# A Fourier stage with one split group, and earlier loads at the start, in a mixed SSM and GLU kernel

## The chip, the cores and the metric

The kernel runs on one core of one Trainium2 chip. The metric is the device time of one execution in microseconds. A core has one matrix engine (TensorE, PE in the profile; PEld is its weight load) and several others that each run their own instructions in order: VectorE (DVE), ScalarE (ACT), GpSimd (POOL) and SyncE (SP). SP issues most of the transfers, POOL the rest.

## The reference

Two branches work on the same 2048 tokens of width 512 in fp32, each on its own input, and a gate per token mixes them. Branch A is a diagonal state-space model, evaluated as a convolution of length 2048 with a kernel K per channel through Fourier transforms of length 4096. Branch B is a bilinear gated linear unit (GLU) with F = 1792.

```python
def _A_ref(u, log_A_real, A_imag, C_real, C_imag, log_dt, D_skip):   # u: 1 x 2048 x 512, N = 128
    dt = jnp.exp(log_dt)
    A = -jnp.exp(log_A_real) + 1j * A_imag
    C = (C_real + 1j * C_imag) * dt[:, None]
    P = jnp.exp((A * dt[:, None])[:, :, None] * pos[None, None, :])
    K = 2.0 * jnp.einsum("dn,dnl->dl", C, P).real
    Kf, Uf = jnp.fft.rfft(K, 2 * L), jnp.fft.rfft(u_t, 2 * L)
    y = jnp.fft.irfft(Uf * Kf[None, :, :], 2 * L)[:, :, :L]
    return y.transpose(0, 2, 1) + u * D_skip[None, None, :]

def _B_ref(x, w_gate, w_up, w_down):                                 # 512 -> 1792 -> 512
    h = jnp.einsum("bsd,df->bsf", x, w_gate) * jnp.einsum("bsd,df->bsf", x, w_up)
    return jnp.einsum("bsf,fd->bsd", h, w_down)

g = _sigmoid((A_u * gate_w).sum(-1, keepdims=True))
return g * _A_ref(A_u, ...) + (1 - g) * _B_ref(B_x, ...)
```

## The kernel before

**The GLU.** F is cut into 14 blocks of 128, in four groups of 3, 3, 4 and 4 (`GROUPS`). The tokens stand in four columns `ci` of 512. The loop `glu` (L650) goes through the groups, and in each through the columns, up and down by turns. `hidden` makes for each block the products `pg` and `pu` (weights `w_gate` and `w_up` in `whi`, `wlo`) and multiplies them to `h`; `down` multiplies `h` with `w_down` (`dhi`, `dlo`) into `y`; `evacuate` scales `y` by one minus the gate into `acc` on ACT and stores it. Each fp32 number is split in a high and a low part of the faster fp32r format, and each product is three matmuls of 128x128 by 512 columns: `dhi,hl`, `dlo,hh`, `dhi,hh` for `y`, and one with `wlo` and two with `whi` for `pg` and `pu`. The high part is a cast on ACT, the low part a subtraction on DVE. There are 2016 such large matmuls in all. The `w_down` rows of the first group come in three transfers into a tile `kt`.

**Tokens.** In the first group, `tokens` (L520) loads a column's tokens x^T in four pieces `kt`, splits them into `xs`, and stores the split tile to DRAM (`xs_d`) for the later groups, which read it from there. For columns 0 and 1 the test at L664 calls `ahead` (L530) first: it loads the four pieces into two staging tiles `ts`, column 1 from planner time 12 on. Columns 2 and 3 come through the rotating buffer `raw`.

**The convolution.** `u_part` (L691) loads u in four tiles of 1 MB (`in<-in_u`). From each, DVE makes four scores (`y,gate<-in,w3s`, which add up to the gate's input, ACT taking their sigmoid) and the sums for a first Fourier stage. Its results go to DRAM (`su_d`) and come back in another layout for the second stage. DVE and ACT also make tables of powers (`x`, `rt`, `v`) from which PE makes K (k block). `m_second` (L1157) is the second stage: for each of four quarters q of the channels and T = 0 to 3 it fills four PSUM banks with 32x32 by 512-column matmuls, for four row groups `r` (the 32 partitions that hold the operand) and four column groups `c` (the 32 output partitions). For T = 0 and c = 0 each row group's matmul is cut in two halves of 256 columns, one for each p, since the second half needs the weight matrix of index 4 (the insert at L109). Then ACT or DVE empties the banks (`ev`), DVE multiplies the spectra, and two more stages go back. The convolution's matmuls all write tiles named `k` and come in bursts between the large ones. In the trace a burst's fp32 matmul has two records.

**The order.** Nothing is issued as it is written. `add` (in the class `Work`, L170) records a task with its engine, a modelled duration, a rank, the tiles it reads and writes, an earliest time `after` and the size of its transfer. `run` (L268) then simulates all engines: again and again it takes the task with the earliest modelled start, and the tasks are emitted in that order. `InOrder` makes each engine run strictly in it. So a change of one `after` or one duration can change every engine's order from there on, and the chip then keeps to the new order whatever the real times are. L124 is the helper that issues everything, so every row of the profile has that line and the tiles' names tell the rows apart.

Of the kernel before, what the change touches and what calls it, by code (L numbers as in the profile page):

```python
# [10 lines left out]
F32 = mybir.dt.float32  # L11
# [7 lines left out]
P = 128  # L19
# [119 lines left out]
U_STEP = 20.0  # L139
# [185 lines left out]
def gated_mix_kernel(  # L325
# [16 lines left out]
    pe, dve, act, sp, pool_q = (InOrder(tc, e) for e in (nc.tensor, nc.vector, nc.scalar, nc.sync, nc.gpsimd))  # L342
# [3 lines left out]
    add = work.add  # L346
# [173 lines left out]
    def tokens(gi, ci, kt):  # L520

        x = xs[kt] = new("glu", "xs", [P, 2, D], F32R, 5)
        if gi:
            add("sp", 0.42, lambda: sp.dma_start(x.t.bitcast(F32), xs_d[ci, kt]), r=[(m_xs, (ci, kt))], w=[x], dma=512, rank=0)
            return
        load(("x", gi, ci, kt), xT[kt * P : (kt + 1) * P, ci * D : (ci + 1) * D])
        split(x, x, (0, 1), ("x", gi, ci, kt))
        add("sp", 0.42, lambda: sp.dma_start(xs_d[ci, kt], x.t.bitcast(F32)), r=[x], w=[(m_xs, (ci, kt))], dma=512, rank=2)

    def ahead(ci):  # L530

        ts = [load_two(lambda k, n=n: ("x", 0, ci, 2 * n + k), stage, None, False) for n in range(2)]
        for kt in range(KT):
            t, k = ts[kt // 2], kt % 2
            src = xT[kt * P : (kt + 1) * P, ci * D : (ci + 1) * D]
            add("sp", 0.42, lambda t=t, k=k, src=src: sp.dma_start(t.t[:, k], src), w=[(t, k)], dma=256, after=12.0 if ci == 1 else 0.0)

    THREE = ((1, 0), (0, 1), (0, 0))

# [110 lines left out]
    def glu():  # L650
        order = [(gi, ci) for gi in range(len(GROUPS)) for ci in (range(4) if gi % 2 == 0 else range(3, -1, -1))]
        tokens(0, 0, 0)
        weights(GROUPS[0])
        first = new("tab", "kt", [P, 4, D])
        for f in GROUPS[0]:
            raws[("w", f, 2)] = (first, f)
            src = wts[f][:, 2 * D :]
            add("sp", 0.42, lambda f=f, src=src: sp.dma_start(first.t[:, f], src), w=[(first, f)], dma=256, after=9.0 if f == 2 else 0.0)
        down_weights(GROUPS[0])
        old = 0  # L660
        for n, (gi, ci) in enumerate(order):
            fs = GROUPS[gi]
            if ci != old:
                if gi == 0 and ci <= 1:  # L664
                    ahead(ci)
                for kt in range(KT):
                    tokens(gi, ci, kt)
            old = ci
            hs = {f: hidden(f) for f in fs}
            ends = n % 4 == 3 and gi + 1 < len(GROUPS)  # L670
            if ends:
                weights(GROUPS[gi + 1])

            for rr in ((0, 1), (2, 3)):
                ys = {r: new("ps_y", "y", [P, D], bufs=2) for r in rr}
                late = fs[-1:] if rr[0] == 0 else []
                for r in rr:
                    for f in fs:
                        if f not in late:
                            down(ys[r], r, hs[f], wd[f], f == fs[0], f == fs[-1])  # L680
                    if not late:
                        evacuate(gi, ci, r, ys[r])
                if late:
                    for r in rr:
                        down(ys[r], r, hs[fs[-1]], wd[fs[-1]], False, True)
                        evacuate(gi, ci, r, ys[r])
            if ends:
                down_weights(GROUPS[gi + 1])


    def u_part(t):  # L691
        ut = inp([P, 4, D])
        rs = slice(4 * t, 4 * t + 4)
        add("sp", 0.42, lambda: sp.dma_start(ut.t, uv[:, rs, :]), w=[ut], dma=1024, after=9.0 + U_STEP * t)

        def score_of(j):
            r = 4 * t + j
            pr = new("mid", "y", [P, D], bufs=2)
            add(
                "dve", 0.73,  # L700
                lambda: dve.scalar_tensor_tensor(
                    pr.t, ut.t[:, j, :], 1.0, gw.t, op0=ALU.mult, op1=ALU.mult, accum_out=gate[:, r : r + 1]
                ),
                r=[ut, gw], w=[pr, (m_gate, ("s", t))], rank=0,
            )

        for j in range(4):
            score_of(j)
        ones = [new("mid", "y", [P, 2, D], bufs=2) for _ in range(2)]
        ops = (ALU.add, ALU.subtract)  # L710
        for y, op in zip(ones, ops):
            add(
                "dve", 1.22,
                lambda y=y, op=op: dve.tensor_tensor(out=y.t, in0=ut.t[:, :2], in1=ut.t[:, 2:], op=op), r=[ut], w=[y],
            )
        for s, op in enumerate(ops):
            for d, y in enumerate(ones):
                add(
                    "dve", 0.69,
                    lambda d=d, s=s, y=y, op=op: dve.tensor_tensor(  # L720
                        out=ut.t[:, 2 * s + d], in0=y.t[:, 0], in1=y.t[:, 1], op=op
                    ),
                    r=[y], w=[(ut, 2 * s + d)],
                )

        def first(s):
            banks, st = [bank() for _ in range(4)], new("mid", "ev", [P, KT, 4, P], bufs=2)

            def fn():
                for p in range(2):  # L730
                    col, src = 64 * (p + s), 2 * s + (p + s) % 2
                    for tq in range(4):
                        lanes = slice(32 * tq, 32 * tq + 32)
                        pe.matmul(
                            banks[tq].t[64 * p : 64 * p + 64], w1_t.t[lanes, col : col + 64], ut.t[lanes, src],
                            start=True, stop=True, tile_position=(32 * tq, 64 * p),
                        )

            add("pe", 1.3, fn, r=[(ut, 2 * s), (ut, 2 * s + 1), w1_t], w=banks, rank=1, hold=[st])
            for tq in range(4):  # L740
                add(
                    "act", 0.59,
                    lambda tq=tq: act.copy(st.t[:, :, tq], banks[tq].t.rearrange("p (f d) -> p f d", f=KT)),
                    r=[banks[tq]], w=[(st, tq)],
                )
            n0 = 16 * s + 4 * t
            for q in range(KT):
                add(
                    "pool", 0.95,
                    lambda q=q: pool_q.dma_start(  # L750
                        su_d[q, :, n0 : n0 + 4, :], st.t[:, q],
                    ),
                    r=[st], w=[(m_su, (q, n0))], dma=256,
                )

        for s in range(2):
            first(s)
        sc, ga = (m_gate, ("s", t)), (m_gate, t)
        add("act", 1.5, lambda: act.activation(gate[:, rs], gate[:, rs], AF.Tanh, scale=0.5), r=[sc], w=[sc], rank=0)

        def gates():
            dve.tensor_scalar(ngate[:, rs], gate[:, rs], -0.5, 0.5, op0=ALU.mult, op1=ALU.add)
            dve.tensor_scalar(gate[:, rs], gate[:, rs], 0.5, 0.5, op0=ALU.mult, op1=ALU.add)

        add("dve", 0.4, gates, r=[sc], w=[ga, sc], rank=0)
# [391 lines left out]
    def m_second(q, T, ins, w):  # L1157

        banks = [bank() for _ in range(4)]
        to = new("mid", "ev", [P, 2, 2, 2, 2 * P], bufs=2)  # L1160
        at, parts = ins

        def fn():
            src = at().rearrange("l (p c) w d -> l c p (w d)", p=2)
            for c in range(4):
                for r in range(4):
                    lanes, to = slice(32 * r, 32 * r + 32), banks[r].t[32 * c : 32 * c + 32]
                    pieces = [(c, to, src[lanes, c])]
                    if T == 0 and c == 0:

                        pieces = [(4 * p, to[:, 2 * P * p : 2 * P * p + 2 * P], src[lanes, c, p]) for p in range(2)]
                    for m, to, x in pieces:
                        pe.matmul(to, w.t[lanes, m], x, start=True, stop=True, tile_position=(32 * r, 32 * c))

        add("pe", 1.05, fn, r=[*parts, w], w=banks, rank=1, hold=[to], many=apart_of(q))
        for r in range(4):
            h, e = divmod(r, 2)
            evict(
                q, r, 0.59, lambda h=h, e=e: to.t[:, :, e, :, P * h : P * h + P],
                lambda r=r: banks[r].t.rearrange("l (p w d) -> l w p d", p=2, w=2), [banks[r]], [(to, r)],  # L1180
            )
        return to
# [268 lines left out]
```

## Time and profile before

| quantity | value |
|---|---|
| median of 3 runs | 595.36 us (594.47 to 596.06) |
| the profiled execution | 595.34 us |
| its span in the profile | 593.6 us |
| mean granted TensorE clock | 0.996 |
| PE busy | 579.7 us |
| DVE, ACT, POOL busy | 512.1, 401.8, 113.7 us |

The span runs from the first to the last instruction of the profile; the time has 1.7 us around it. A timeline row gives the start, the duration, the engine, the line, the operation with output and inputs, the shape, the count of like instructions in one row, and in brackets the idle time before it with what ended it. Busy times overlap, since matmuls are pipelined, so the pace of PE is read from starts and not from durations. The granted clock is the share of the full TensorE clock.

### The profile page before, as it was taken

To read this page: it belongs to the slowest core of one execution; us is meant where nothing else is said; L and a number is where in the kernel's file an instruction comes from. 1 tells how busy PE (TensorE), PEld (TensorE's weight loads), DVE (VectorE), ACT (ScalarE), POOL (GpSimd) and SP (SyncE) were. 2 spreads that over 40 slices of the span, in tenths; PEclk is the share of its full clock that TensorE was granted. 3 is DMA by queue.
4 is the path that set the end of the run, shared out by engine and by line. 5 is a ranking of instruction groups with operands and counts; after the bars stand their busy time and mean duration, and the time that the engine had idled before them with its cause. 6 is when DMAs were issued, how large, how long until landed. Compare 5 with 4: busy or idle time off the path is not lost.

```text
span 593.6 us, 14891 instructions
## 1 busy us (share of the span) xinstructions
PE 579.7 (98%) x6020; PEld 436.6 (74%) x6020; DVE 512.1 (86%) x812; ACT 401.8 (68%) x891; POOL 113.7 (19%) x159
## 2 busy tenths in 40 slices
PE   8899999999999999899999999999999899999996
PEld 5677676788877777687676877867877776777764
DVE  6998999999998999899999999996999972556845
ACT  5348898898679488878887675799786343433351
POOL 0003212411111231310123201112422104202011
PEclk9989999999999999999999999999999999999999
DMA  8998779896867697998789856899969349898887
GB/s 270 408 368 299 273 274 347 199 309 197 204 178 204 203 239 189 227 267 263 153 200 264 188 149 190 177 279 260 225 137 251 68 131 252 271 285 207 262 187 132
DMA packets 71687, 136.28 MB, mean 230 GB/s; under 512 B 6852, under 2 KB 35780, under 8 KB 69188
## 3 DMA queue, kind: packets, MB, share of 16 engines
q1 hardware_dynamic: 47668, 87.10, 43.0%
q0 software_dynamic: 23392, 47.98, 38.6%
q8 instruction: 47, 0.77, 0.5%
q10 hardware_dynamic: 560, 0.26, 0.2%
q14 instruction: 20, 0.16, 0.1%
HBM read 80.27 MB, written 55.05 MB: 228 GB/s over the span
## 4 chain that ended last, share of the span: by engine, by line
PE 90%; DVE 5%; issue 2%; ACT 2%; DMA 1%; DVEq 0%; SPq 0%; ACTq 0%
PE pg L124 25%; PE y L124 24%; PE pu L124 24%; PE k L124 16%; DVE x L124 1%; DMA y<-in_xT 1%; DVE v L124 1%; DVE wlo L124 1%; DVE in L124 0%; ACT acc L124 0%; DMA raw<-in_xT 0%; DVE h L124 0%; DVE dlo L124 0%; ACT L124 0%; ACT xs L124 0%
## 5 line engine op out<-in xcount | busy, mean ns | idle before, releaser
L124 PE MATMUL pg<-xs,whi 128*128 128x512 f32 x448 | 139.0, 391 | 0.5 <-ACT whi L124 0.5
L124 PE MATMUL pu<-xs,whi 128*128 128x512 f32 x448 | 138.6, 391 | 0.0
L124 PEld LDWEIGHTS pg<-xs,whi 128*128 128x128 f32 x448 | 84.4, 188 | 20.9 <-ACT whi L124 2.1
L124 PEld LDWEIGHTS pu<-xs,whi 128*128 128x128 f32 x448 | 84.4, 188 | 17.0
L124 PE MATMUL y<-dhi,hl 128*128 128x512 f32 x224 | 89.7, 400 | 4.3 <-ACT acc L124 2.2
L124 PE MATMUL pg<-xs,wlo 128*128 128x512 f32 x224 | 89.8, 401 | 2.2 <-issue 1.6
L124 PE MATMUL pu<-xs,wlo 128*128 128x512 f32 x224 | 90.3, 403 | 0.0
L124 PE MATMUL y<-dlo,hh 128*128 128x512 f32 x224 | 87.7, 391 | 0.2 <-DVE dlo L124 0.2
L124 PE MATMUL y<-dhi,hh 128*128 128x512 f32 x224 | 87.5, 391 | 0.0
L124 ACT COPY ev<-k 128x512 f32<-128x512 f32 x112 | 59.4, 599 | 22.6 <-PE k L124 22.5
L124 POOL DMA_DIRECT2D out<-acc x44 | 39.4, 972 | 154.9 <-ACT acc L124 150.3
L124 ACT CAST hh<-h 128x512 fp32r<-128x512 f32 x56 | 34.9, 623 | 45.7 <-DVE h L124 45.0
L124 PEld LDWEIGHTS y<-dhi,hl 128*128 128x128 f32 x224 | 42.0, 188 | 26.8 <-issue 10.6
L124 ACT ACTIVATE acc<-y,ngate 128x512 f32<-128x512 f32 x62 | 42.2, 690 | 27.5 <-PE y L124 24.4
L124 PEld LDWEIGHTS pu<-xs,wlo 128*128 128x128 f32 x224 | 42.1, 188 | 20.9 <-issue 10.5
L124 DVE TENSOR_TENSOR h<-pu,h 128x512 f32<-128x512 f32 x56 | 38.6, 690 | 21.6 <-PE pu L124 19.9
L124 PEld LDWEIGHTS pg<-xs,wlo 128*128 128x128 f32 x224 | 42.3, 189 | 17.0 <-issue 6.2
L124 ACT COPY h<-pg 128x512 f32<-128x512 f32 x56 | 33.0, 590 | 24.6 <-PE pg L124 18.2
L124 PEld LDWEIGHTS y<-dhi,hh 128*128 128x128 f32 x224 | 42.2, 188 | 9.1
L124 PEld LDWEIGHTS y<-dlo,hh 128*128 128x128 f32 x224 | 42.1, 188 | 8.6 <-DVE dlo L124 0.5
L124 DVE TENSOR_TENSOR hl<-h,hh 128x512 fp32r<-128x512 f32 x56 | 38.4, 686 | 4.0 <-ACT hh L124 3.9
L124 POOL DMA_DIRECT2D su_d<-ev x32 | 17.9, 577 | 94.4 <-ACT ev L124 94.4
(130 smaller groups left out, 985.4 us busy)
## 6 DMA issues: line engine op xcount, KB each, us to landing
xs<-xs_d SPq DMA_DIRECT2D x36, 512.0 KB, 6.1
out<-acc POOLq DMA_DIRECT2D x44, 256.0 KB, 5.4
raw<-in_wts SPq DMA_DIRECT2D x33, 256.0 KB, 6.1
xs_d<-xs SPq DMA_DIRECT2D x16, 512.0 KB, 6.0
su_d<-ev POOLq DMA_DIRECT2D x32, 256.0 KB, 6.7
y_d<-ts SPq DMA_DIRECT2D x28, 256.0 KB, 6.0
in<-su_d POOLq DMA_DIRECT2D x12, 512.0 KB, 7.7
sk_d<-ev SPq DMA_DIRECT2D x6, 1024.0 KB, 5.7
```

The costliest lines, as they stand in the source:

```text
L124: got = getattr(self.engine, name)(*args, **kw)
```

## The change

The change has four parts.

- In `m_second` with T = 0, only the first matmul, row group 0 and column group 0, is split. Its half p = 0 (weights 0) comes first, then the 15 whole ones, and its half p = 1 (weights 4) last. The burst has 17 matmuls in place of 20. For T = 1 to 3 nothing changes.
- The stores of column 0's split tokens to `xs_d` may start from planner time 16 + kt on.
- `ahead` is called for column 2 too, from time 42 on; its tokens then go through `ts` and not `raw`.
- The four loads of u may start at 6, 27, 48 and 69 in place of 9, 29, 49 and 69.

```diff
-        add("sp", 0.42, lambda: sp.dma_start(xs_d[ci, kt], x.t.bitcast(F32)), r=[x], w=[(m_xs, (ci, kt))], dma=512, rank=2)
+        add("sp", 0.42, lambda: sp.dma_start(xs_d[ci, kt], x.t.bitcast(F32)), r=[x], w=[(m_xs, (ci, kt))], dma=512, rank=2, after=16.0 + kt if ci == 0 else 0.0)
...
-            add("sp", 0.42, lambda t=t, k=k, src=src: sp.dma_start(t.t[:, k], src), w=[(t, k)], dma=256, after=12.0 if ci == 1 else 0.0)
+            add("sp", 0.42, lambda t=t, k=k, src=src: sp.dma_start(t.t[:, k], src), w=[(t, k)], dma=256, after=12.0 + 30.0 * (ci - 1))
...
-                if gi == 0 and ci <= 1:
+                if gi == 0 and ci <= 2:
                     ahead(ci)
...
-        add("sp", 0.42, lambda: sp.dma_start(ut.t, uv[:, rs, :]), w=[ut], dma=1024, after=9.0 + U_STEP * t)
+        add("sp", 0.42, lambda: sp.dma_start(ut.t, uv[:, rs, :]), w=[ut], dma=1024, after=6.0 + (U_STEP + 1.0) * t)
...
-            for c in range(4):
-                for r in range(4):
-                    lanes, to = slice(32 * r, 32 * r + 32), banks[r].t[32 * c : 32 * c + 32]
-                    pieces = [(c, to, src[lanes, c])]
-                    if T == 0 and c == 0:
-
-                        pieces = [(4 * p, to[:, 2 * P * p : 2 * P * p + 2 * P], src[lanes, c, p]) for p in range(2)]
-                    for m, to, x in pieces:
-                        pe.matmul(to, w.t[lanes, m], x, start=True, stop=True, tile_position=(32 * r, 32 * c))
+            jobs = [(r, c, c, slice(0, 2)) for c in range(4) for r in range(4)]
+            if T == 0:
+
+                jobs = [(0, 0, 0, 0), *jobs[1:], (0, 0, 4, 1)]
+            for r, c, m, p in jobs:
+                lanes = slice(32 * r, 32 * r + 32)
+                to = banks[r].t[32 * c : 32 * c + 32].rearrange("l (p d) -> l p d", p=2)[:, p]
+                pe.matmul(to, w.t[lanes, m], src[lanes, c, p], start=True, stop=True, tile_position=(32 * r, 32 * c))
```

The first place is the start. SP's issues there before, from the second `v` load on (`kt` is the first group's `w_down`, `in` is u's tile, `ts` the second column's tokens, `dt_d` a small table in DRAM):

```order
L124 DMA v<-in_prm 128x1024
L124 DMA kt<-in_wts 128x512 x2
L124 DMA xs_d<-xs 128x1024 x4
L124 DMA in<-in_u 128x2048
L124 DMA kt<-in_wts 128x512
L124 DMA ts<-in_xT 128x512 x4
L124 DMA dt_d<-small 128x4
L124 DMA in<-in_u 128x2048
```

and after the change:

```order
L124 DMA v<-in_prm 128x1024
L124 DMA in<-in_u 128x2048
L124 DMA kt<-in_wts 128x512 x3
L124 DMA ts<-in_xT 128x512 x4
L124 DMA dt_d<-small 128x4
L124 DMA xs_d<-xs 128x1024 x4
L124 DMA x<-dt_d 128x512
L124 DMA in<-in_u 128x2048
```

The four stores of column 0 moved behind u's first tile, all of `kt` and the second column's tokens. DVE at the same place before, from the second block's `hl` on (`x` is the table of powers, `y,gate` a score):

```order
L124 TENSOR_TENSOR hl<-h,hh 128x512
L124 TENSOR_TENSOR dlo<-kt,dhi 128x512 x2
L124 SCALAR_TENSOR_TENSOR x<-x 128x512 x3
L124 TENSOR_TENSOR h<-pu,h 128x512
L124 SCALAR_TENSOR_TENSOR x<-x 128x512 x2
L124 TENSOR_TENSOR hl<-h,hh 128x512
L124 SCALAR_TENSOR_TENSOR x<-x 128x512
L124 SCALAR_TENSOR_TENSOR y,gate<-in,w3s 128x512 x2
L124 TENSOR_TENSOR dlo<-kt,dhi 128x512
```

and after:

```order
L124 TENSOR_TENSOR hl<-h,hh 128x512
L124 SCALAR_TENSOR_TENSOR x<-x 128x512 x3
L124 SCALAR_TENSOR_TENSOR y,gate<-in,w3s 128x512
L124 SCALAR_TENSOR_TENSOR x<-x 128x512
L124 SCALAR_TENSOR_TENSOR y,gate<-in,w3s 128x512
L124 TENSOR_TENSOR dlo<-kt,dhi 128x512
L124 SCALAR_TENSOR_TENSOR y,gate<-in,w3s 128x512
L124 TENSOR_TENSOR dlo<-kt,dhi 128x512
L124 SCALAR_TENSOR_TENSOR y,gate<-in,w3s 128x512
L124 TENSOR_TENSOR dlo<-kt,dhi 128x512
L124 TENSOR_TENSOR h<-pu,h 128x512
L124 TENSOR_TENSOR xs<-ts,xs 128x512
```

The scores moved ahead of the `dlo`, and the first `dlo` now stands behind four `x` and two scores; the third block's `h` and `hl` stand behind all three `dlo`. The second place is the first T = 0 burst on PE, before:

```order
L124 MATMUL pu<-xs,whi 128x512 x2
L124 MATMUL k<-in,w2s 32x256 x8
L124 MATMUL k<-in,w2s 32x512 x12
L124 MATMUL pu<-xs,wlo 128x512
L124 MATMUL pu<-xs,whi 128x512 x2
```

and after:

```order
L124 MATMUL y<-dhi,hh 128x512
L124 MATMUL k<-in,w2s 32x256
L124 MATMUL k<-in,w2s 32x512 x15
L124 MATMUL k<-in,w2s 32x256
L124 MATMUL y<-dhi,hl 128x512
```

The three other row groups lost their halves, the remaining two stand at the burst's ends, and the burst itself stands between other large matmuls. The third place is ACT where the first quarter's second stage is nearly done (T = 2 and 3, about 240 us), before (`ev` empties the banks, `whi` and `wlo` are weights of the next group, `acc` empties `y`):

```order
L124 CAST whi_2966<-raw_2879 128x512
L124 COPY ev_2946<-k_2921 128x2x2x128
L124 CAST whi_2966<-raw_2886 128x512
L124 ACTIVATE rt_2762<-rt_2762,fixed_82 128x672
L124 ACTIVATE wlo_2991<-whi_2966 128x1024
L124 ACTIVATE acc_3017<-y_2942,ngate_84 128x512
L124 ACTIVATE acc_3021<-y_2956,ngate_84 128x512
```

and after:

```order
L124 CAST whi_2964<-raw_2883 128x512
L124 COPY ev_2960<-k_2924 128x2x2x128
L124 COPY ev_2960<-k_2926 128x2x2x128
L124 COPY ev_2960<-k_2928 128x2x2x128
L124 ACTIVATE acc_2985<-y_2915,ngate_84 128x512
L124 CAST whi_2964<-raw_2900 128x512
L124 ACTIVATE acc_2999<-y_2956,ngate_84 128x512
L124 ACTIVATE wlo_3008<-whi_2964 128x1024
```

The two `acc` moved ahead of `wlo`, the first of them also ahead of the second `whi`.

## The prediction

> **What bounds the kernel now.** I read the page's busy times and chain first, then TensorE's waits.
>
> ```profile
> span 593.6 us, 14891 instructions
> PE 579.7 (98%) x6020; PEld 436.6 (74%) x6020; DVE 512.1 (86%) x812; ACT 401.8 (68%) x891; POOL 113.7 (19%) x159
> PE 90%; DVE 5%; issue 2%; ACT 2%; DMA 1%; DVEq 0%; SPq 0%; ACTq 0%
> ```
>
> TensorE (PE) is busy for 98% of the span and is 90% of the chain that ended last. Every microsecond by which it works less, waits less, or runs at a higher clock is a microsecond of the kernel. Next, the waits of PE: releaser, total, times, longest.
>
> ```profile
> PE y L124 <- ACT acc L124: 2.2, 2, 1.5
> PE y L124 <- ACT dhi L124: 2.0, 1, 2.0
> PE pg L124 <- issue: 1.6, 1, 1.6
> PE k L124 <- DVE acc L124: 1.5, 1, 1.5
> PE pg L124 <- ACT whi L124: 1.0, 2, 0.5
> PE k L124 <- DVE v L124: 0.4, 1, 0.4
> PE y L124 <- DVE dlo L124: 0.2, 1, 0.2
> ```
>
> They come to 8.9 us. `dhi` and `dlo` stand at the start, one `acc` of 1.5 in the middle; the first row of `k` and `whi` lie before the place where the orders part.
>
> The busy time itself can shrink too. Here are two second-stage bursts on PE's timeline, with the matmul behind each, the weight loads of the first, and the last burst of its kind.
>
> ```profile
> 201.45 2.13 PE L124 MATMUL k<-in,w2s 32*32 32x256 f32 x40
> 203.51 0.50 PE L124 MATMUL pu<-xs,wlo 128*128 128x512 f32 x1
> 209.87 1.14 PE L124 MATMUL k<-in,w2s 32*32 32x512 f32 x32
> 210.94 0.50 PE L124 MATMUL y<-dhi,hl 128*128 128x512 f32 x1
> ...
> 201.44 1.23 PEld L124 LDWEIGHTS k<-in,w2s 32*32 32x32 f32 x40 [0.35 <-issue]
> ...
> 528.23 2.14 PE L124 MATMUL k<-x,w2s 32*32 32x256 f32 x40
> ```
>
> Two records are one matmul. With T = 0 (20 matmuls) PE moves on after 203.51 − 201.45 = 2.06 us; with T = 1 (16) after 1.07. The four T = 0 bursts, 2.13 to 2.14 long in the records, are alike.
>
> Last, the start: PE's timeline, and two windows (columns PE, PEld, DVE, ACT, POOL busy, granted clock, DMA share, GB/s).
>
> ```profile
> 23.26 0.39 PE L124 MATMUL y<-dhi,hl 128*128 128x512 f32 x1
> ...
> 25.75 0.39 PE L124 MATMUL y<-dhi,hh 128*128 128x512 f32 x1
> 28.10 0.50 PE L124 MATMUL y<-dhi,hl 128*128 128x512 f32 x1 [1.96 <-ACT dhi L124]
> 28.82 0.50 PE L124 MATMUL y<-dlo,hh 128*128 128x512 f32 x1 [0.22 <-DVE dlo L124]
> ...
> 33.03 0.39 PE L124 MATMUL pg<-xs,wlo 128*128 128x512 f32 x1
> ```
>
> ```profile
> 30.00:34.00 4.00, 4.00 (x13) 3.12 (x13) 3.97 (x9) 2.24 (x6) 0.00 (x0) 0.63 0.88 310
> 240.00:250.00 10.00, 8.45 (x65) 6.03 (x64) 8.67 (x11) 9.85 (x18) 3.47 (x4) 1.00 0.84 210
> 20.00:22.00 2.00, 2.00 (x11) 1.65 (x10) 2.00 (x4) 1.15 (x3) 0.00 (x0) 1.00 1.03 422
> ```
>
> Twelve matmuls start from 23.26 to 25.75: (25.75 − 23.26)/11 = 0.227 us each, the full pace. Thirteen start from 25.75 until just before 33.03. They should take 13 × 0.227 = 2.95 and take 7.28, so the start loses 4.3 us. Of that, 1.96 + 0.22 are waits and some 2.0 the lowered clock after them (0.63 in the window from 30 to 34). At 244, a wait of 1.5 left the clock at 1.00.
>
> **The second stage.** The edit removes three of 20 matmuls in each T = 0 burst and moves the second half of the split group to the end. Before, each half's partner on the same tile of the array follows directly. The work of a row group is the same for T = 0 and T = 1 (two halves and three wholes against four wholes), so the 0.99 us of difference are four such pairs, 0.25 each. After the edit no pair is adjacent. Row group 0 runs half a matmul ahead of the others through the middle, and the closing half fills that up. Lower bound: 1.07, as T = 1. Upper bound: the closing half still waits as a pair does and then runs alone as long again, 1.07 + 2 × 0.25 = 1.57. In proportion to matmuls it would be 1.07 + 0.99/4 = 1.32. I take 1.15, a third of a pair's wait over T = 1, because the halves are 15 matmuls apart and nearest to the T = 1 row. Four bursts: 4 × (1.15 − 2.06) = **−3.6 us**, between −4.0 and −2.0. Nothing hides them: PE works on its chain there.
>
> On weights, the row of loads shows all 40 within 1.23 us, while matmuls on the same row groups run until 203.5. [...]
>
> **The start.** SyncE's (SP) issues, the DMA summaries (landings of `kt`; of `in`, median of two), and what VectorE (DVE) and ScalarE (ACT) do with what lands:
>
> ```profile
> 9.85 1.59 SPq L124 DMA_DIRECT2D kt<-in_wts  x2
> 13.30 2.77 SPq L124 DMA_DIRECT2D xs_d<-xs  x4
> 16.13 0.45 SPq L124 DMA_DIRECT2D in<-in_u  x1
> 17.26 0.33 SPq L124 DMA_DIRECT2D kt<-in_wts  x1
> 17.91 3.71 SPq L124 DMA_DIRECT2D ts<-in_xT  x4
> ...
> DMA to landing us min/median/max: 7.4/8.0/10.1
> ...
> in<-in_u SPq DMA_DIRECT2D x2, 1024.0 KB, 10.6
> ```
>
> ```profile
> 19.84 0.69 DVE L124 TENSOR_TENSOR hl<-h,hh 128x512 fp32r<-128x512 f32 x1
> 20.44 1.29 DVE L124 TENSOR_TENSOR dlo<-kt,dhi 128x512 fp32r<-128x512 f32 x2
> 21.64 2.14 DVE L124 SCALAR_TENSOR_TENSOR x<-x 128x512 f32<-128x512 f32 x3
> ...
> 26.84 0.69 DVE L124 SCALAR_TENSOR_TENSOR y<-in,w3s 128x512 f32<-128x512 f32 x1
> ...
> 27.43 0.62 ACT L124 CAST dhi<-kt 128x512 fp32r<-128x512 f32 x1 [2.39 <-DMA kt<-in_wts]
> ```
>
> The third `kt` load is issued at 17.26, behind four stores of 512 KB and u's tile, lands 10.1 later, and PE's 1.96 wait follows. After the change, SP issues u's tile, three `kt`, four `ts`, and only then the stores. The first `kt` landed at 9.85 + 8.0 = 17.9. With u's 1 MB in its place at 422 GB/s (2.5 us in place of 0.6), u lands at about 19.8, the three `kt` at 20.4, 21.1 and 21.7, the `ts` by 24.4. These are estimates from the rows above. ACT then casts the three `dhi` by about 22.5, in time for PE at 23.26, and the wait of 1.96 is gone.
>
> DVE is late next, since its order changes. After `hl` it now does three `x`, a score (`y<-in,w3s`), an `x`, a score, and only then the first `dlo`. At 0.61 per step from row to row (26.84 to the next score, and a third of what two `dlo` and three `x` take) and 0.69 for the last: 20.44 + 3 × 0.69 = 22.5 for the `x`, 24.3 for score, `x` and score, and 24.33 + 0.69 = 25.02 for `dlo`. PE wants it at 23.49, its second matmul, and gets it at 25.07: wait 1.58. The second `dlo` ends at 26.24, in time for 25.07 + 6 × 0.227 = 26.43. PE reaches the next column's products at 27.56 and their low part at 27.79, but DVE's `xs` split ends at about 28.7 (score, `dlo`, `h`, `xs` after 26.16): wait 0.92. The third block's `hl` ends at about 30.2 and costs 0.42. In all 2.92 against 4.3: **−1.4 us**. The longest of these waits is near the 1.5 that left the clock alone at 244, so I count no lowered clock. If only the first wait stays, it is −2.7; if the clock falls as it did at 28, costing 2.0, it is +0.6.
>
> The moved stores cost PE nothing so long as their reader is far: the view of the tile `xs_d` gives
>
> ```profile
> L124 SPq DMA_DIRECT2D xs<-xs_d x36: 319/326/1101, 90.6 to 532.3; - x36
> ```
>
> so the first read back is at 90.6, 60 us behind, and it is column 2's; column 0 comes last of that group. The later u tiles move from 29, 49, 69 to 27, 48, 69 in the planner's time; the third column's four loads keep their bytes and change only the buffer. From 33 to 89 PE has no wait, so neither can gain there. What a loss would be is in the next term.
>
> **The middle.** The planner gives new orders to every engine from the start on, so the waits there are drawn again. The largest, 1.5 at 244, is `acc` standing behind casts on ACT:
>
> ```profile
> 242.43 1.04 ACT L124 ACTIVATE wlo<-whi 128x1024 fp32r<-128x1024 f32 x1
> 243.38 1.25 ACT L124 ACTIVATE acc<-y,ngate 128x512 f32<-128x512 f32 x2
> ```
>
> There both `acc` now stand ahead of `wlo`, and the first also ahead of the second `whi`, so 1.04 of the 1.5 goes. One return from small matmuls to the large ones falls away (PE's order has 61 stretches of products against 62): the rows behind a burst, at 203.51 and 210.94, are 0.50 long against 0.39 in the stream, and I take twice that difference, 0.2. Against this I set one new wait about the size of the other one for `acc` (2.2 − 1.5 = 0.7). Together −1.0 − 0.2 + 0.6 = **−0.7 us**. Bounds: −2.4, all `acc` waits and the switch gone; +1.6, one more wait like the largest. The 1.6 under "issue" waits for nothing that the profile shows; I leave it.
>
> **The sum.** −3.6 − 1.4 − 0.7 = −5.7. The profiled execution took 595.34 (span 593.6 and 1.7 around it), as the median of the runs, 595.36. Forecast: **589.6 us**.
>
> **The rivals.**
>
> *The closing half waits.* The second stage gives −2.0: 591.3. For it: four pairs do cost 0.25 each. Against: the loads' row. Chance 0.12.
>
> *The pauses at the start lower the clock.* Waits of 1.58, 0.92 and 0.42 come within 7 us. For it: 1.96 and 0.22 lowered it at 28. Against: 1.5 at 244 did not. 589.6 + 2.0 = 591.6. [...] Chance 0.15.
>
> *The middle takes the gain back.* Three or four new waits of 1.5 behind casts or loads, as at 244: 594 to 596. For it: DVE is 86% busy and every order is new. Against: before shows only one of that size. Chance 0.09, no measurable difference.
>
> *Slower: DVE waits for u.* The first score now stands ahead of the first `dlo` on DVE and needs u's tile by 22.5. Each microsecond by which u lands later is one of PE's, and 2.0 more for the clock: at 26.7, where u landed before (16.13 + 10.6), 589.6 + 4.2 + 2.0 = 595.8, no faster than before; from 28.1 on it is over 597.15. For it: 10.6 from issue to landing in the summary. Against: issued at 9.85, the same 10.6 ends at 20.5, and the stores no longer stand ahead. Chance 0.06.
>
> **How the numbers follow.** The forecast keeps 0.58. A difference under 0.3% (1.8 us) can't be told from none: 593.57 to 597.15 is the same. Faster: 0.58 + 0.12 + 0.15, less 0.01 for overlaps, 0.84. Same: 0.09 and that 0.01, 0.10. Slower: 0.06. The terms' bounds, taken as independent (−0.4/+1.6, −1.3/+2.0, −1.7/+2.3), make about −2.2/+3.4 around 589.6: **587.0 to 593.0**, which holds the first two rivals and leaves out the last two, 0.15.
>
> **What would show it.** Second stage right: T = 0 bursts followed after 1.07 to 1.3 us; wrong: 1.5 or more. Start right: no wait for `dhi` near 28, one of about 1.6 for `dlo` near 25, clock at 1.00 to 34, and the first small first-stage burst at about 36.4, after 117 large matmuls (before: 39.25, after 123). Wrong: u landing after 22.5, or a window near 30 under 1.00. Middle right: the wait at the third round under 0.6 and PE's waits from 80 on at 3 to 4 us in all; over 7 there would make the forecast wrong.

## The result, and the profile after

The changed kernel takes 591.52 us in the median of eight runs (589.96 to 592.85), and the kernel before 596.54 beside it (594.14 to 598.65). The ratio is 0.9918 with a 95% interval of 0.9895 to 0.9941. The profiled execution took 592.45, with a span of 590.6.

The busy times and the chain of the changed kernel's page:

```profile
span 590.6 us, 14844 instructions
PE 576.8 (98%) x5996; PEld 435.3 (74%) x5996; DVE 512.5 (87%) x812; ACT 400.0 (68%) x891; POOL 113.6 (19%) x159
PE 85%; DVE 9%; ACT 2%; issue 2%; DMA 1%; DVEq 0%; SPq 0%; ACTq 0%
```

PE is busy for 2.9 us less. DVE's share of the chain rose from 5% to 9% here, but it is 3% in a second profile of the same kernel, so nothing is read from it. PE's waits (total, times, longest):

```profile
PE k L124 <- DVE v L124: 3.0, 1, 3.0
PE k L124 <- DVE acc L124: 1.5, 1, 1.5
PE y L124 <- issue: 1.5, 1, 1.5
PE y L124 <- DVE dlo L124: 1.4, 1, 1.4
PE pg L124 <- ACT whi L124: 1.0, 2, 0.5
PE pg L124 <- DVE xs L124: 0.6, 1, 0.6
```

The waits for `dhi` and for ACT's `acc` are gone. In their place stand one of 1.4 for `dlo` (0.2 before), one of 0.6 for `xs`, and one of 3.0 for `v` (0.4 before). Now the places of the prediction, on PE's timeline of the changed kernel: the start, the wait for `v`, and the first T = 0 burst.

```profile
23.24 0.39 PE L124 MATMUL y<-dhi,hl 128*128 128x512 f32 x1
25.03 0.50 PE L124 MATMUL y<-dlo,hh 128*128 128x512 f32 x1 [1.40 <-DVE dlo L124]
...
28.66 0.73 PE L124 MATMUL pg<-xs,whi 128*128 128x512 f32 x2 [0.60 <-DVE xs L124]
...
36.52 1.11 PE L124 MATMUL k<-in,w2s 32*64 32x512 f32 x16
...
140.94 0.39 PE L124 MATMUL y<-dhi,hh 128*128 128x512 f32 x1
144.28 3.12 PE L124 MATMUL k<-v,x 128*32 128x64 f32 x128 [2.95 <-DVE v L124]
147.33 0.80 PE L124 MATMUL y<-dhi,hl 128*128 128x512 f32 x1
...
205.65 1.14 PE L124 MATMUL k<-in,w2s 32*32 32x256 f32 x34
206.72 0.50 PE L124 MATMUL y<-dhi,hl 128*128 128x512 f32 x1
```

The T = 0 burst is followed after 206.72 − 205.65 = 1.07 us, as all four are, in place of 2.06. The burst of K at 144.28 waits 2.95 and then takes 3.05 until its successor, where others of its kind take 2.00. The windows of the changed kernel (last three columns: granted clock, DMA share, GB/s) show what was different there:

```profile
30.00:34.00 4.00, 3.95 (x18) 3.17 (x18) 4.00 (x6) 2.30 (x4) 0.00 (x0) 1.00 0.94 320
141.00:144.00 3.00, 0.33 (x2) 0.00 (x0) 3.00 (x6) 2.42 (x5) 0.86 (x1) 1.00 0.92 307
144.00:148.00 4.00, 3.72 (x130) 3.49 (x131) 3.42 (x9) 0.56 (x2) 0.00 (x0) 0.63 1.06 328
```

The clock stays up at the start, and falls to 0.63 behind the wait for `v`. Between the last product and that burst DVE works without a pause (`ri` and `sq` belong to the tables for K):

```profile
139.72 0.85 DVE L124 TENSOR_TENSOR ri<-rt,e 128x672 f32<-128x672 f32 x1
140.49 0.68 DVE L124 TENSOR_TENSOR h<-pu,h 128x512 f32<-128x512 f32 x1
141.09 0.68 DVE L124 TENSOR_TENSOR v<-v,sq 128x512 f32<-128x512 f32 x1
141.69 0.85 DVE L124 TENSOR_TENSOR ri<-t,e 128x672 f32<-128x672 f32 x1
142.46 0.68 DVE L124 TENSOR_TENSOR hl<-h,hh 128x512 fp32r<-128x512 f32 x1
143.06 0.61 DVE L124 SCALAR_TENSOR_TENSOR v<-v 128x256 f32<-128x256 f32 x1
143.52 0.62 DVE L124 TENSOR_TENSOR v<-v,sq 128x256 f32<-128x256 f32 x1
```

### The profile page after: what moved, and what is told of

Same layout as the page of the kernel before. It is cut to its first block, busy times and chain, and to the rows that moved or that the text cites. A ratio compares the mean times of both kernels' runs of the same rounds, so it can differ in the third digit from the quotient of the medians.

```text
span 590.6 us, 14844 instructions
## 1 busy us (share of the span) xinstructions
PE 576.8 (98%) x5996; PEld 435.3 (74%) x5996; DVE 512.5 (87%) x812; ACT 400.0 (68%) x891; POOL 113.6 (19%) x159
## 4 chain that ended last, share of the span: by engine, by line
PE 85%; DVE 9%; ACT 2%; issue 2%; DMA 1%; DVEq 0%; SPq 0%; ACTq 0%
PE y L124 25%; PE pg L124 23%; PE pu L124 22%; PE k L124 16%; DVE v L124 2%; DVE x L124 2%; DVE hl L124 1%; DMA y<-in_xT 1%; DVE h L124 1%; DVE wlo L124 1%; DVE ri L124 1%; DVE m L124 1%; DVE t L124 0%; DVE y L124 0%; ACT ev L124 0%
## 5 line engine op out<-in xcount | busy, mean ns | idle before, releaser
L124 PEld LDWEIGHTS k<-v,x 128*32 128x32 f32 x2048 | 31.7, 111 | 8.8 <-issue 7.8
```

What stands on the lines that cost most here:

```text
L124: got = getattr(self.engine, name)(*args, **kw)
```

## The experiments

Two questions were open: how much of the gain is the split's, and what makes the new wait. The first theory for the wait was that DVE is full from 60 to 165 and simply can't deliver `v` sooner. Its rival was that the planner held products back by their earliest times, so that PE reached the burst too soon.

**The split alone, and everything but the split.** The first kernel is before with the diff's last part only (every engine keeps its order); the second is the changed kernel with the old lines of that part.

> Before with the new split alone; every engine keeps its order. Both theories: the four T = 0 bursts are followed after 1.07 us in place of 2.06, so 4.0 us less than before, about 592.5 where before is at 596.5. The start keeps its 1.96 wait and its lowered clock, and there is no wait of 3 us near 141. If this kernel is level with the changed one, the other three parts together are worth about 1 us.

> The changed kernel with the old split (20 matmuls); its order is the changed one's. Both theories: 4.0 us more than the changed kernel, so 1 us under before (595.5 where before is at 596.5), with the wait of 3 us near 141. If the loss near 141 cancels the start entirely, it is level with before or above it.

Measured: the split alone took 592.37 against 595.30, ratio 0.9962 (0.9940 to 0.9984). That is 2.3 us less (1.0 to 3.6), short of the 4.0 expected (a second comparison below gave 3.5), though all four of its T = 0 bursts are followed after 1.07. The wait for `dhi` was 1.6 and the clock did not fall behind it, where 1.96 and a fall were expected. The changed kernel with the old split took 594.64, ratio 0.9992 (0.9975 to 1.0010): no difference from before that can be measured. Its T = 0 bursts are at 2.07 again, and the wait for `v` is there, 2.9. The clock stays at 1.00 behind that wait.

**The blocks' earliest times 5 us sooner.**

```diff
-        after = T_STEP * len(steps) - 5.0
+        after = T_STEP * len(steps) - 10.0
```

> The changed kernel with the earliest times of the blocks' products 5 us sooner (T_STEP x step - 10 in place of - 5), so that six more large matmuls stand ahead of the third burst of K. Pacing theory (the products held back by those times alone make PE wait near 141): the wait of 3.0 and the lowered clock behind it go, 4 to 5 us less than the changed kernel. DVE theory (DVE is full from 60 to 165 and sets when the table v is ready, near 144): the burst still starts near 144, the wait shrinks by 6 x 0.227 = 1.4 to about 1.6, short enough to keep the clock, 1.4 to 3.3 us less than the changed kernel.

Measured: 591.07 against 595.30, ratio 0.9940 (0.9916 to 0.9964), not to be told from the changed kernel, where both theories had 1.4 us or more less. In its profile and in that of the kernel with the old split the first small burst starts at 38.09 and 38.11 us, so the two can be compared at the burst of K. (In the changed kernel's profile that first burst started at 36.52.) PE's timeline with the old split, and then with the earlier times, each row cut off where the view ends:

```profile
145.84 0.37 PE L124 MATMUL k<-v,x 128*32 128x64 f32 x10 [2.93 <-DVE v L124]
```

```profile
145.84 1.38 PE L124 MATMUL k<-v,x 128*32 128x64 f32 x82 [0.70 <-DVE v L124]
```

The burst starts at the same time to the hundredth, with six more large matmuls ahead of it. So the six products only fill the wait, and the rival falls so far: the end of `v` sets the burst.

**Less work for DVE near 95.**

```diff
+        cut = 8 if t == 3 else D
...
-                lambda y=y, op=op: dve.tensor_tensor(out=y.t, in0=ut.t[:, :2], in1=ut.t[:, 2:], op=op), r=[ut], w=[y],
+                lambda y=y, op=op: dve.tensor_tensor(out=y.t[:, :, :cut], in0=ut.t[:, :2, :cut], in1=ut.t[:, 2:, :cut], op=op), r=[ut], w=[y],
```

(and the same cut in the four sums behind these two).

> The changed kernel with DVE's six sums over u's fourth tile (near 95) done on 8 of 512 columns; the rest of those sums is left out, and every engine keeps its order. DVE theory: DVE is 4 to 5 us sooner from 97 on, v is ready near 140, PE does not wait for it near 141, the clock stays at 1.00, and the time is 4 to 5 us under the changed kernel. If another releaser (a transfer or GpSimd) sets v, the third burst stays near 144 and the time within 1 us of the changed kernel.

Measured: 591.97 against 595.30, ratio 0.9948 (0.9926 to 0.9970): no gain, and the wait for `v` is still 2.80. DVE's timeline of this kernel shows where the freed time went:

```profile
93.65 0.39 DVE L124 TENSOR_TENSOR in<-y 128x8 f32<-128x8 f32 x4
96.97 0.69 DVE L124 TENSOR_TENSOR h<-pu,h 128x512 f32<-128x512 f32 x1 [2.92 <-PE pu L124]
...
136.31 0.69 DVE L124 TENSOR_TENSOR h<-pu,h 128x512 f32<-128x512 f32 x1 [1.54 <-PE pu L124]
```

DVE reached the next block's `h` sooner and waited 2.92 for PE there, where it had waited 0.26. From 97 to 134 DVE's steps start within 0.1 us of the changed kernel's. But PE stood still for 1.45 us for no event that the profile shows (131.28 to 132.73), DVE waited 1.54 for it at the next `h`, and from that `h` to the burst it is 9.50 us in both kernels. So the first theory falls in its plain form too: time that DVE gains is lost again at an `h`, where it needs PE's product, and a stop of PE moves both engines. What counts is what stands on DVE between such an `h` and the end of `v`. In the changed kernel DVE has next to no idle time from 115 to 144. PE's `pu` for the last `h` ends near 140, DVE comes to that `h` half a microsecond later, and `h`, a `v`, `ri`, `hl` and two more `v` follow, 140.49 to 144.14. PE has only six matmuls left for that time.

**Shorter steps behind that `h`.** The last four steps of the third block's `v` go over 2 of 32 channels.

```diff
+            few = 2 if b == 2 else TB
...
-                    dst[1](), src[0](), 2.0, src[1](), op0=ALU.mult, op1=ALU.mult
+                    dst[1]()[:, :few], src[0]()[:, :few], 2.0, src[1]()[:, :few], op0=ALU.mult, op1=ALU.mult
```

> The changed kernel with the last four DVE steps of the third block's table v (two products, two differences, two of them between the block's h at 140.5 and the burst at 144.3) done on 2 of 32 channels, the rest left out; every order is kept. If the wait near 141 is DVE's work standing between that h and the end of v: three of the four steps lie behind h, 0.5 + 0.35 + 0.45 less, the burst starts 1.3 us sooner, the wait is 1.7 in place of 3.0, and the time 1.3 us under the changed kernel, 3 where the clock then stays. If DVE's whole load since 97 counts, 1.9 us sooner by all four steps. If something else ends the wait, no change.

Measured: 590.80 against 595.64, ratio 0.9932 (0.9905 to 0.9959), which is not to be told from the changed kernel, so the gain of 1.3 us in time is not shown. PE's timeline:

```profile
140.85 0.39 PE L124 MATMUL y<-dhi,hh 128*128 128x512 f32 x1
143.22 2.05 PE L124 MATMUL k<-v,x 128*32 128x64 f32 x128 [1.99 <-DVE v L124]
```

The burst starts 1.0 sooner (1.3 by the steps behind `h`, 1.9 by all four). DVE's timeline shows the rest. The step ahead of `h` is 0.5 shorter, but `h` then waits 0.25 for ACT and so starts only 0.2 sooner. The last step of `v` waits 0.41 for `sq`, which ACT makes. That bears out the steps behind `h`: what was gained ahead of it was mostly lost at it.

**What the halves cost.** Both kernels are before with another list of matmuls for T = 0: all 20 with the halves apart, and the new 17 with the halves as neighbours. Each ran once, so the bursts are read and not the times (589.60 and 593.38).

```diff
-                jobs = [(0, 0, 0, 0), *jobs[1:], (0, 0, 4, 1)]
+                jobs = [(r, 0, 0, 0) for r in range(4)] + jobs[4:] + [(r, 0, 4, 1) for r in range(4)]
```

```diff
-                jobs = [(0, 0, 0, 0), *jobs[1:], (0, 0, 4, 1)]
+                jobs = [(0, 0, 0, 0), (0, 0, 4, 1), *jobs[1:]]
```

> Before with 20 matmuls in each T = 0 burst as before, but the four first halves at the burst's head and the four second halves at its end, so that no two halves of one tile are neighbours. If neighbours cost (0.25 per pair): the burst is followed after 1.07 to 1.15 us. If the count of matmuls costs (0.25 for each past the 16th): after 2.06.

> Before with the new split's 17 matmuls, but the second half directly behind the first. If neighbours cost: 1.07 + 0.25 = 1.32 us, so 1.0 us in all four bursts more than with the half at the end. If only the count costs: as with the half at the end, 1.07 or a little above.

PE's timeline with the halves apart, and with the two as neighbours:

```profile
199.61 1.29 PE L124 MATMUL k<-in,w2s 32*32 32x256 f32 x40
200.83 0.50 PE L124 MATMUL pu<-xs,wlo 128*128 128x512 f32 x1
```

```profile
201.59 1.44 PE L124 MATMUL k<-in,w2s 32*32 32x256 f32 x34
202.96 0.50 PE L124 MATMUL pu<-xs,wlo 128*128 128x512 f32 x1
```

Twenty matmuls take 1.22 with the halves apart and 2.06 as four pairs: a pair of neighbours costs (2.06 − 1.22)/4 = 0.21. Seventeen take 1.37 with one pair and 1.07 with none, 0.30. All four bursts of each profile give the same figures to 0.01. So 0.84 of the 0.99 was the neighbours; the four extra matmuls themselves cost 0.15.

**The other parts.** One kernel leaves out the third column's staging, the other has only it and the split (the diff's second and third parts, and its last).

> The changed kernel without the third column's staging (its tokens come through raw, as before); the split, the later stores and the earlier u are kept, all orders are planned anew. If the staging makes the wait near 141: no wait over 1 us between 130 and 150, and 3 to 5 us less than the changed kernel. If any early start makes it, since the tables of K on DVE and ACT set the pace from 97 on: a wait of 2 to 4 us on v or on h between 125 and 150, and level with the changed kernel within 1.5 us.

> Before with the new split and the third column's staging; stores and u as before. If K's tables set the pace from 97 on and an early start only arrives there too soon, this kernel (start as before: the 1.96 wait for dhi) has no wait over 1 us between 100 and 165 and lies within 1 us of the changed kernel, 4 to 5 us under before. If the earlier start is worth its 1.8 us at the end, it lies 2 us over the changed kernel, 3 us under before.

Measured: without the staging 595.60 against 595.64, ratio 1.0000 (0.9973 to 1.0027); with only it and the split 598.55 against 595.22, ratio 1.0054 (1.0032 to 1.0075). Both expectations missed. The first kernel was to lie at most 1.5 us over the changed one, and by the ratios to before (0.9918 and 0.9942 for the changed kernel) it lies 3.5 to 4.9 over it. The second was to lie at most 2 us over it and lies 6.8 over (591.73 in the same comparison). PE's longest waits without the staging:

```profile
PE k L124 <- issue: 2.2, 1, 2.2
PE k L124 <- DVE v L124: 1.7, 1, 1.7
PE y L124 <- DVE hl L124: 1.6, 2, 1.4
...
```

and with only it and the split:

```profile
PE k L124 <- issue: 5.9, 2, 3.9
...
```

In the first the wait for `v` is 1.7, and others of the same kind stand beside it (on `hl`, near 116). So an early start does make such waits with or without the staging. But they do not explain the time: PE's last matmul starts at 586.24 there and at 585.52 in the changed kernel, so PE is only 0.7 us later, where the spans differ by 3.1 (593.7 and 590.6). The other 2.4 lie behind PE's last matmul, where the span goes on for 7.5 us in place of 5.1. POOL issues the last two stores of the convolution's result (`out<-x`, 512 and 256 KB) at 582.3 and 584.0, in the changed kernel in one row from 579.0 on, and the last stores behind them take 4.7 to 5.0 us from issue to landing in place of 2.8. In the second kernel there is no wait over 1 us on DVE or ACT from 100 to 165, as expected; but a burst of K stands still for 3.9 us, two records before its end, for no event that the profile shows. The other 2.0 is in a burst near 345. The end of this kernel is late too: the span goes on for 8.7 us behind PE's last matmul. Its profiled execution (602.54) is the longest of its eleven runs, so these sizes are above the usual.

**The changed kernel beside the split alone, and a version with other times.** The last one has the blocks' earliest times 5 us sooner and the third column from 37 on.

```diff
-        after = T_STEP * len(steps) - 5.0
+        after = T_STEP * len(steps) - 10.0
...
-            add("sp", 0.42, lambda t=t, k=k, src=src: sp.dma_start(t.t[:, k], src), w=[(t, k)], dma=256, after=12.0 + 30.0 * (ci - 1))
+            add("sp", 0.42, lambda t=t, k=k, src=src: sp.dma_start(t.t[:, k], src), w=[(t, k)], dma=256, after=12.0 + 25.0 * (ci - 1))
```

> The changed kernel again, beside the others of this call: 4.9 us under before (0.9918). Its wait of 3 us near 141 and its 1.6 us near 23 stay; the lowered clock behind the first may be absent.

> The split alone, beside the changed kernel. By its bursts 4.0 us under before. If the other three parts are worth anything together, the changed kernel lies under it, by 0.7 us from the kernel with the old split (1 us expected).

> The changed kernel with the blocks' earliest times 5 us sooner and the third column's tokens from 37 on in place of 42. If the wait near 141 can be filled with products that were held back: 1.4 us or more under the changed kernel, with a wait under 1.5 us there. If the tables on DVE and ACT only take the time elsewhere between 97 and 165: within 1 us of the changed kernel.

Measured, beside one another and against 595.22: the changed kernel 591.73, ratio 0.9942 (0.9919 to 0.9965); the split alone 591.75, ratio 0.9941 (0.9916 to 0.9966); the version with other times 590.15, ratio 0.9927 (0.9892 to 0.9962). The first two are level: the other three parts are worth nothing together that could be measured (each ratio is known to some 0.0025, 1.5 us). In the third, the wait for `v` is gone. Its waits on PE, and DVE's steps before the burst, which starts at 142.68:

```profile
PE k L124 <- DVE acc L124: 1.5, 1, 1.5
PE y L124 <- DVE dlo L124: 1.4, 1, 1.4
PE y L124 <- ACT acc L124: 0.9, 1, 0.9
PE pg L124 <- ACT whi L124: 0.9, 2, 0.5
PE pg L124 <- DVE xs L124: 0.6, 1, 0.6
PE pg L124 <- ACT h L124: 0.5, 1, 0.5
```

```profile
139.56 0.85 DVE L124 TENSOR_TENSOR ri<-t,e 128x672 f32<-128x672 f32 x1
140.33 0.62 DVE L124 SCALAR_TENSOR_TENSOR v<-v 128x256 f32<-128x256 f32 x1
140.82 0.69 DVE L124 TENSOR_TENSOR h<-pu,h 128x512 f32<-128x512 f32 x1
141.43 0.63 DVE L124 TENSOR_TENSOR v<-v,sq 128x256 f32<-128x256 f32 x1
```

Here one step of `v` stands behind `h` in place of three, and `ri` and `hl` no longer stand between. DVE is no less full: from 97 to 144 it is busy for 46.3 of 47 us, against 45.9 in the changed kernel. Only three more large matmuls stand ahead of the burst (513 against 510), yet it starts 1.6 us sooner. So the wait was not filled with products, as one expectation had it: `v` is ready sooner, by the order of DVE's steps and not by their sum. The span of the profiled execution is 584.9, the shortest of all, but it is also the shortest of the kernel's seven runs (587.02 to 594.53), and the intervals of the ratios do not tell it from the changed kernel.

## Why the prediction was right, and where it was not

The time, 591.5, lies in the range of 587.0 to 593.0, and the direction was right. It moved by 4.9 us in the first comparison (596.54 × 0.0082) and by 3.5 in the second (595.22 × 0.0058), where 5.7 was forecast. Of the three terms the second stage gave a little more than forecast, the start less on the whole, and the middle cost time where a gain was forecast. In the profiles the spans differ by 3.0 us; with 4.0 from the second stage and 1.3 from the start, some 2.3 were lost elsewhere, beyond the bound of +1.6 that the middle was given. That the time still lies in the range is in part luck: with one of the four parts left out (no staging of the third column) the new orders gave 595.60, above it. Two slips of the working are small: with its own 0.7 for the new wait the middle is −1.0 − 0.2 + 0.7 = −0.5 and not −0.7, and 589.6 − 2.2 is 587.4 and not 587.0.

*The second stage.* Forecast −3.6, from 1.15 per burst; measured 1.07, so 4 × 0.99 = −4.0, the lower end of that term. The argument held: neighbours on one tile cost (0.21 to 0.30 a pair, above), and the closing half adds nothing (17 matmuls take 1.07, as 16 whole ones do). That it fills a lead of its row group is the author's explanation, and no row shows such a lead. The forecast gave a third of a pair's wait to a half 15 matmuls away; it has none. The first rival, the closing half that waits, falls: the burst takes no longer than one of 16 whole matmuls, 1.07, and the row of its 34 weight loads is 0.56 long. What the 0.21 to 0.30 for neighbours is made of was not shown: these runs do not separate a waiting weight load from a waiting matmul.

*The start.* The step-by-step walk came out close: `dlo` at 25.03 against 25.07, the split of `xs` at 28.66 against 28.7, the first small burst at 36.52 after 117 large matmuls against 36.4. From 23.24 to 33.03 the changed kernel has 30 matmuls, 30 × 0.227 = 6.8, so it loses 3.0 where 2.9 was forecast, and 4.3 in before's profile: −1.3 for −1.4. What was wrong is to take 4.3 as what before loses. In the two profiles of the split alone, which has before's orders, the wait for `dhi` is 1.6 and 2.0, the clock stays at 1.00 from 28 to 34, and up to the first small burst, with 0.227 taken off for each large matmul ahead of it, they take 0.2 to 0.3 us less than the changed kernel. So the changed start is worth its 1.3 us only in executions in which the clock would have fallen; in the others it costs 0.2 to 0.3. Of six profiles with the old start, three show the fall; of eight with the new, none does. The second rival had the clock fall in the changed kernel, and it fell only with the old start.

*The moved stores and the third column.* The forecast let them cost nothing, as PE had no wait from 33 to 89 that they could touch. But they gave every engine another order: without the staging the kernel takes some 4 us more, and the sum of all parts but the split is nil (0.9942 against 0.9941).

*The middle.* Forecast −0.7, with one new wait of 0.7; this is the step that failed. The wait near 244 went wholly (no row of ACT's `acc` is left, −1.5, where −1.0 was forecast). Not all of this is the change's: of the two profiles of the split alone, with before's order, one has this wait (1.7) and one has not. The new wait is 3.0, and with the clock's fall it cost 2.95 + 1.05 + 0.5 in the profiled execution. The 0.5 is on the large matmuls behind the burst, up to the start of the fourth, against the kernel with the old split, which has the same order there and kept its clock. At 165.45 both kernels start the fourth burst of K, the changed one with 585 large matmuls done and the old one with 597: 12 × 0.227 = 2.7 us behind, with its lead of the start gone. The test given for it, PE's waits from 80 on at 3 to 4 us in all, came out at 4.4, plus the clock. The wait was there to be read: in the changed order of DVE, `ri`, `hl` and three steps of `v` stand behind the `h` of the last block before the burst. The prediction looked for what a wait could cost and not for where one stands.

*The slower rival* did not come up: u's tile was there for the first score, as the first `dlo` was not later than the forecast.

## What to carry to other kernels

Halves that use the same tile of the matrix engine one directly behind the other cost about a quarter of a microsecond a pair here, with one pair in the burst (0.30) and with four (0.21 each); putting other tiles' work between them gave 0.84 of the 0.99 us per burst, without a single matmul less. An earlier start is worth only what the next meeting point leaves of it: in a kernel in which two engines meet at every block, look in the new order at what stands between the last such meeting and the step that a third party waits for. And a change that makes a planner draw all orders anew should be priced by the split part and the rest apart, since the rest moves by several microseconds either way for reasons that are in none of its lines.

## What the runs showed of the hardware

Whether the clock falls behind a wait differs from one execution to the next. The same wait for `v`, 2.8 to 3.0 us, lowered the clock in two of four profiles (0.63 from 144 to 148 in one, 0.51 from 144 to 147 in the other) and left it at 1.00 in the two others. In these two the wait began 1.6 to 1.7 us later (at 142.9 and 143.0 against 141.3); whether that decided it, the runs do not show. At the start, waits of 1.96 and 0.22 lowered the clock in before's profile, and waits of 1.99 and 0.23 did not in one of the split alone. A fall cost 1.6 us behind the wait for `v` (1.05 + 0.5 above) and some 2.0 at the start.

The first products run slowly too, and not equally long in all executions. In three of the 14 profiles (the kernel with the old split, the one with the earlier times, the one with only the staging and the split) they follow one another at 0.43 us up to about 10.7 and not at 0.227; in the changed kernel's profile the full pace is reached at about 7.3. That is the 1.6 us between 36.52 and 38.11 above, and the windows show a granted clock of 1.00 all the while.

Waits for no event that the profile shows came up at places that differ from kernel to kernel: behind a burst near 463 in before's profile (1.6 us), between large matmuls near 415 in the changed kernel (1.5), inside bursts without the staging (2.2) and in the kernel with only the staging and the split (3.9 and 2.0). In this last kernel PE and the windows show

```profile
109.29 0.27 PE L124 MATMUL k<-v,x 128*32 128x64 f32 x2 [3.91 <-issue]
```

```profile
106.00:109.00 3.00, 0.00 (x0) 0.00 (x0) 0.00 (x0) 1.27 (x2) 0.38 (x1) 1.00 1.07 332
109.00:113.00 4.00, 3.71 (x10) 2.91 (x10) 3.40 (x6) 2.20 (x5) 0.00 (x0) 0.57 0.43 84
```

PE stands still two records before the burst's end, with the transfer engines full (1.07), and loses the clock behind it (0.57). Instructions come by transfers of their own, as this row of the changed kernel's DMA queues shows (packets, MB, share):

```profile
q8 instruction: 47, 0.77, 0.5%
```

That is 16 KB a packet, and one packet for every 255 of PE's 11,992 records (5,996 matmuls and as many weight loads); that they bring PE's instructions is read from this count and from the stops. In the kernel with only the staging and the split one of them began at 106.88, within the long stop, and another at 345.05, 0.35 us before the other stop. The same holds everywhere: the 14 profiles have 22 stops of PE of 0.3 us or more for no event, and each of them ends 2.2 to 2.7 us after one of these packets began (2.41 in before's profile, from 461.10 to 463.50, and 2.42 in the changed kernel's, from 413.63 to 416.06). A burst with 128 records of small matmuls has as many of weight loads, so it uses up 256 in 2.0 us, about a packet's worth. A large matmul uses two in 0.227, so the burst draws them some fourteen times as fast. That PE waits for its instructions in these stops is the author's reading of the timing, which speaks for it in every case; no run took the cause away, and why a packet begins late is open.
